# Retention layer with a routed MLP: another order of work on GpSimd, masks and one-hots on other engines, narrower state products

## The chip, the cores and the metric

The kernel runs on one core of a Trainium2 chip. The metric is device time in microseconds of one execution. The profile is a hardware trace of one execution; its span, from the first to the last instruction, is somewhat shorter than the device time. Five engines work from queues of their own, each in the order in which the program gives it the instructions: TensorE (PE; its weight loads are listed as PEld), VectorE (DVE), ScalarE (ACT), GpSimd (POOL) and SyncE (SP). DMA moves data between device memory and the on-chip buffer.

## What is computed

Four sequences (B = 4) of S = 768 positions with H = 8 heads of D = 64. Each head keeps a 64×64 state that decays by a constant of the head. The result, 512 wide, goes through a mixture-of-depths layer: of each sequence the 128 rows with the highest score pass an MLP (512 to 1024 to 512) and are added back, weighted by a sigmoid of the score; the others are left as they are.

```python
for t in range(S):
    state = gamma * state + k[t] (outer) v[t]          # per batch and head
    y[t] = scale * q[t] @ state
x = y as (B, S, H * D)
scores = x @ w_gate
for b in range(B):
    top = the 128 rows of x[b] with the highest score
    ye = relu(x[b, top] @ w1) @ w2
    out[b] = x[b];  out[b, top] += sigmoid(scores[b, top]) * ye
```

## The kernel before

The recurrence is done in chunks of 128 positions, two chunks to a block, 12 blocks, three to a sequence. Within a chunk the scores q·k are computed at once, masked to the causal half (`am`), and multiplied with v; what comes from earlier chunks is q times the state. The state is accumulated in a PSUM bank (`PS`) and copied to SBUF in bf16 (`St`) after each chunk.

All operations are entered into a plan: each has an engine, an estimated cost, what it reads and what it writes. A list scheduler in plain Python, which runs while the program is built, simulates the plan with these costs and so fixes the order on each engine. The order is static: on the chip nothing is rearranged.

```python
P.dma(0.87, ..., nc.gpsimd.dma_start(kt[:, m], ...))   # q, k, v: 36 loads by GpSimd, float32 to bf16
...
def prep(m):        # per block: kd = k * decay (DVE), transposes of kd and q (PE), their copies (ACT, DVE)
    ...
MASKED = {(m, 1, 1): ("tt" if m % 2 else "aff") for m in range(1, NBL)}   # NBL = 12
def block(m):       # four mask units a block: (half, s)
    f_qk: for hp, r, s, X:                              # 16 products a half, 64 rows x 64 columns each
        matmul(bank[A0 + s][X * 64:(X + 1) * 64, ...], kT[i][s * 64:.., ..64 columns], qT[i][s * 64:.., ..128])
    f_m:  am = bank * mask                              # DVE, all units that aren't in MASKED
    f_mc: am = copy of bank (ACT);  f_mp: am *= mask, or affine_select in two halves (POOL)
    f_kv: for hp, r:                                    # state, 8 products a chunk
        matmul(o[:, hp, :], kd[i][x, r, 2 * hp:2 * hp + 2, :], V[x, 2 * hp:2 * hp + 2, r, :])
    f_se: St = copy of bank[PS], two diagonal halves (ACT)
    f_qs: Y += qT @ St;  f_av: Y += am @ V              # PE
    f_xs: xs = scale * Y (ACT);  f_sc: score = sum(scale * Y * wg) (DVE)
```

In `f_kv` a product has the keys of two heads as its 128 columns and the values of the same two heads as its 128 moving columns, so it gives a 2×2 arrangement of 64×64 blocks of which the two diagonal ones are used.

The selection counts for each row how many rows of its sequence have a higher score (`L`, comparisons on DVE, counts on PE), builds one-hot matrices `OH` from the ranks, gathers the 128 rows with them on PE, and runs the MLP:

```python
def select(b, ...):
    cnt (PE) -> rk (DVE)
    def f_oh():
        e = nc.gpsimd if b < B - 1 else nc.vector
        for c in range(NC):                             # NC = 6
            e.tensor_scalar(OH[b % 2][:, c, :], slots, rk[..., c:c + 1], after[:, c:c + 1],
                            op0=OP.subtract, op1=OP.is_equal)
    ax (PE: row numbers and gates) ; xr (PE: rows) -> XR (ACT) -> transposes (PE) -> XG (ACT)
def mlp(b, ...):
    h (PE) -> hT = relu (ACT) -> ye (PE) -> ot = ye * gate + XR (DVE) -> scatter into out (POOL, indirect DMA)
...
AHEAD = 5           # loads of blocks 1 to 4 first, then one block ahead per block
if m == 0: ld_w("w1", ...); ld_w("w2", ...)             # weights: two loads of 1024 KB (bf16) each
```

Of the kernel before, what the change touches and what calls it, by code (L numbers as in the profile page):

```python
# [27 lines left out]
PE, DVE, ACT, POOL, SP, DMA = "PE", "DVE", "ACT", "POOL", "SP", "DMA"  # L28
LAT = {PE: 0.20, DVE: 0.16, ACT: 0.25, POOL: 0.2, SP: 0.1, DMA: 0.1}


class Op:
    __slots__ = ("i", "eng", "cost", "fn", "deps", "name", "succ", "due", "start", "end")


class Plan:


    def __init__(self):
        self.ops = []  # L40
        self.wr = {}
        self.rd = {}

    def add(self, eng, cost, fn, reads=(), writes=(), name="", due=None, after=()):
# [16 lines left out]
        o.succ = []  # L61
        self.ops.append(o)
# [4 lines left out]
    def dma(self, issue, nbytes, fn, reads=(), writes=(), name="", eng=POOL, rate=0.37, fixed=1.8, due=None):  # L67
        a = self.add(eng, issue, fn, reads=reads, writes=[("iss", name)] + list(writes), name=name, due=due)
        t = self.add(DMA, nbytes / rate / 1e6, None, reads=[("iss", name)], writes=[("fly", name)], name=name + ".x",
                     after=[])  # L70
        self.add("FLY", fixed, None, reads=[("fly", name)] + list(reads), writes=writes, name=name + ".f", after=[t])
        return a
# [6 lines left out]
    def forward(self, prio):  # L79
# [5 lines left out]
        free = {}  # L85
# [6 lines left out]
        while done < n:  # L92
            best = None
            for e, c in cand.items():
                if not c:
                    continue
                f = free.get(e, 0.0)
                if e == "FLY":
                    i = min(c, key=lambda i: ready[i])
                    t = ready[i]  # L100
                else:
                    t0 = max(f, min(ready[i] for i in c))
                    i = min((i for i in c if ready[i] <= t0 + 1e-9), key=lambda i: prio[i])
                    t = max(f, ready[i])
                if best is None or t < best[0]:
                    best = (t, e, i)
# [57 lines left out]
    def order(self, rounds=6, verbose=False):  # L164
        n = len(self.ops)
        tail = [0.0] * n
# [4 lines left out]
        for r in range(rounds):  # L171
            s, e = self.forward(prio)
            m = max(e)
            if verbose:
                print("forward", r, m)
            if best is None or m < best[0] - 1e-9:
                best = (m, s, e)
            prio = self.backward(e)
        m, s, e = best
        self.makespan, self.st, self.en = m, s, e  # L180
        return sorted(range(n), key=lambda i: (s[i], i))
# [3 lines left out]
def kernel(  # L185
# [13 lines left out]
    C = 128  # L199
# [80 lines left out]
    def load_k(m):  # L280
        P.dma(0.87, 2 * C * Dm * 4, lambda: nc.gpsimd.dma_start(kt[:, m], src_ap(k, m)), writes=[("k", m)],  # L281
              name=f"ldk{m}")

    def load_q(m):
        P.dma(0.87, 2 * C * Dm * 4, lambda: nc.gpsimd.dma_start(qt[:, m], src_ap(q, m)), writes=[("q", m)],  # L285
              name=f"ldq{m}")

    def load_v(m):
        P.dma(0.87, 2 * C * Dm * 4, lambda: nc.gpsimd.dma_start(vt[:, m], src_ap(v, m)), writes=[("v", m)],  # L289
              name=f"ldv{m}")  # L290
# [23 lines left out]
    for e, t in ((PE, 2.0), (DVE, .8), (ACT, 2.4), (POOL, 1.3), (SP, 1.0)):  # L314
        P.add(e, t, None, name="boot", due=-1.0)
    load_k(0)
    P.add(POOL, 0.2, c_tn, writes=["tn"], name="tn")
    P.add(POOL, 0.3, c_iota, writes=["jp"], name="jp")
    load_q(0)
    P.add(POOL, 0.94, c_tl, writes=["tl"], name="tl")  # L320
    load_v(0)
    P.add(POOL, 0.3, c_tk, writes=["tk"], name="tk")
# [21 lines left out]
    P.add(DVE, 0.6, c_mask, reads=["tl", "tn"], writes=["mask"], name="mask")  # L344
# [15 lines left out]
    for n in range(NB):  # L360
        P.add(ACT, 8 * .18, c_gk(n), reads=["tn"], writes=[("gk", n)], name=f"gk{n}")
        P.add(ACT, 4 * .37, c_gq(n), reads=["lg", "tl"], writes=[("gq", n)], name=f"gq{n}")
# [3 lines left out]
    for i in range(2):  # L366
        P.add(DVE, 0.4, c_S(i), writes=[("S", i, 0), ("S", i, 1)], name=f"S{i}z")
# [26 lines left out]
    P.add(DVE, 2.0, c_aux, reads=["tk"], writes=[("aux0", b) for b in range(B)], name="aux0")  # L394


    def prep(m):
# [28 lines left out]
        P.add(PE, .45, f_kt, reads=[("kd", i), "ident"], writes=[("b", TK)], name=f"KT{m}")  # L426
        P.add(ACT, .92, f_ke, reads=[("b", TK)], writes=[("kT", i)], name=f"ke{m}")
        P.add(PE, .48, f_qt, reads=[("q", m), "ident"], writes=[("b", TQ)], name=f"QT{m}")
        P.add(DVE, .6, f_qe, reads=[("b", TQ), ("gq", n)], writes=[("qT", i)], name=f"qe{m}")

    MASKED = {(m, 1, 1): ("tt" if m % 2 else "aff") for m in range(1, NBL)}

    def block(m):
# [4 lines left out]
        for half in range(2):  # L438
# [25 lines left out]
            def f_mp(s, ia=ia):  # L464
                def f():
                    if MASKED[m, half, s] == "tt":
                        nc.gpsimd.tensor_mul(am[ia][s].rearrange("p a r t -> p a (r t)"),  # L467
                                             am[ia][s].rearrange("p a r t -> p a (r t)"),
                                             mask.rearrange("p r t -> p (r t)")[:, None, :].to_broadcast([128, 2, 2 * C]))
                    else:  # L470
                        for X in range(2):
                            t = am[ia][s][X * 64:(X + 1) * 64].rearrange("p a r (u i) -> p a r u i", u=2)
                            nc.gpsimd.affine_select(t, t, pattern=[[0, 2], [-1, 2], [1, 2], [2, 64]], base=0,
                                                    channel_multiplier=-2, compare_op=OP.is_ge, fill=0.0)
                return f
            P.add(PE, 0.5, f_qk, reads=[("kT", i), ("qT", i)], writes=[("b", A0), ("b", A1)], name=f"qk{m}.{half}")
            for s in range(2):
                if (m, half, s) in MASKED:
                    P.add(ACT, 0.493, f_mc(s), reads=[("b", A0 + s)], writes=[("am", ia, s)], name=f"mc{m}.{half}{s}")
                    P.add(POOL, .95, f_mp(s), reads=[("am", ia, s), "mask"], writes=[("am", ia, s)],  # L480
# [5 lines left out]
        for X in range(2):  # L486
# [3 lines left out]
            def f_kv(X=X, c=c):  # L490
                o = bank[PS].rearrange("p (a x) -> p a x", a=HP)
                x = slice(X * P2, (X + 1) * P2)
                for hp in range(HP):
                    for r in range(2):
                        nc.tensor.matmul(o[:, hp, :], kd[i][x, r, 2 * hp:2 * hp + 2, :], V[x, 2 * hp:2 * hp + 2, r, :],  # L495
                                         start=(c == 0 and hp == 0 and r == 0), stop=False, skip_group_check=True)

            def f_se(s, c=c):
                def f():
                    nc.scalar.activation(  # L500
                        St[c % 2][s * 64:(s + 1) * 64, :, s, :],
                        bank[PS].rearrange("p (a s e) -> p a s e", a=HP, s=2)[s * 64:(s + 1) * 64, :, s], AF.Copy)
# [6 lines left out]
            if c:  # L509
                P.add(PE, .24, f_qs, reads=[("qT", i), ("S", (c - 1) % 2, 0), ("S", (c - 1) % 2, 1)],  # L510
                      writes=[("b", Y0 + X)], name=f"qs{j}")
            if c < NC - 1:
                P.add(PE, 0.46, f_kv, reads=[("kd", i), ("v", m)], writes=[("b", PS)], name=f"kv{j}")
                for s in range(2):
                    P.add(ACT, .28, f_se(s), reads=[("b", PS)], writes=[("S", c % 2, s)], name=f"se{j}.{s}")

        for half in range(2):
            for s in range(2):
# [13 lines left out]
                P.add(PE, 0.24, f_av, reads=[("am", ia, s), ("v", m)], writes=[("b", Y0), ("b", Y1)],  # L532
# [14 lines left out]
    def srow(js, bk):  # L547
# [6 lines left out]
        P.add(PE, n * .13, f, reads=[("sc", j) for j in js] + ["identf"], writes=[("b", bk)], name=f"sr{js[0]}")  # L554
# [6 lines left out]
        for a, j in enumerate(js):  # L561
# [6 lines left out]
            P.add(DVE, .08 + (c + 1) * .133, h, reads=[("SR", b % 2, cc) for cc in range(c + 1)] + [("sc", j), "tri"],  # L568
# [14 lines left out]
    def select(b, cnt, axb, xrb, xgb):  # L583
# [7 lines left out]
        P.add(PE, 21 * .05, f_cnt, reads=[("L", c) for c in range(NC)] + ["tri"], writes=[("b", cnt)], name=f"cnt{b}")  # L591
# [6 lines left out]
        def f_oh():  # L598
            e = nc.gpsimd if b < B - 1 else nc.vector
            for c in range(NC):  # L600
                e.tensor_scalar(OH[b % 2][:, c, :], slots, rk[b % 2][:, c:c + 1], after[:, c:c + 1],  # L601
                                        op0=OP.subtract, op1=OP.is_equal)
        P.add(POOL if b < B - 1 else DVE, 1.6 if b < B - 1 else .98, f_oh, reads=[("rk", b % 2), "slots", "after"], writes=[("OH", b % 2)], name=f"oh{b}")
# [5 lines left out]
        P.add(PE, .3, f_aux, reads=[("OH", b % 2), ("aux", b)], writes=[("b", axb)], name=f"ax{b}")  # L609
# [18 lines left out]
        P.add(PE, 1.35, f_xr, reads=[("OH", b % 2)] + [("xs", b * NC + c) for c in range(NC)], writes=[("b", xrb)],  # L628
# [15 lines left out]
    def mlp(b, hb, yb):  # L644
        for s in range(2):
# [6 lines left out]
            P.add(PE, .92, f_h, reads=[("XG", b % 2), "w1"], writes=[("b", hb[s])], name=f"h{b}.{s}")  # L652
# [5 lines left out]
        for s in range(2):  # L658
# [3 lines left out]
            P.add(PE, .88, f_y, reads=[("hT", b % 2, s), "w2"], writes=[("b", yb)], name=f"ye{b}.{s}")  # L662
# [3 lines left out]
        P.add(DVE, .62, f_o, reads=[("b", yb), ("g", b), ("XR", b)], writes=[("ot", b)], name=f"o{b}")  # L666
# [16 lines left out]
    def store(j0, n):  # L683
        b, c = divmod(j0, NC)

        def f():
            for r in range(2):
# [7 lines left out]
        P.dma(1.1, n * C * Dm * 4, f, reads=[("xs", j) for j in range(j0, j0 + n)], writes=[("out", b, c)],  # L695
              name=f"st{j0}")

    def ld_w(name, t, src, n, rows):
        P.dma(1.0, 128 * n * rows * 4, lambda: nc.gpsimd.dma_start(
            t, bass.AP(tensor=src.tensor, offset=src.offset, ap=[[rows, 128], [128 * rows, n], [1, rows]])),  # L700
            writes=[name], name="ld" + name)


    AHEAD = 5
    for m in range(1, AHEAD):
        load_block(m)
    prep(0)
    for m in range(NBL + 1):
# [3 lines left out]
        if m < NBL:  # L712
            block(m)
            if m + AHEAD < NBL:
                load_block(m + AHEAD)
            if m == 0:
# [59 lines left out]
```

## Time and profile before

| | |
|---|---|
| device time, median of 2 runs (lowest to highest) | 132.25 us (131.7 to 132.8) |
| span of the profiled execution | 129.8 us |
| DMA packets | 42753, 19.38 MB |
| loads of q, k and v | 36 issues of 256 KB (bf16), about 11 us each from issue to landing |
| loads of the weights | 2 issues of 1024 KB (bf16), 15.8 us |
| stores of the unchanged rows | 6 of 768 KB and 6 of 256 KB |
| mean granted TensorE clock | 0.828 |
| GpSimd: issues of the 36 loads | 32.9 us busy |
| GpSimd: one-hots, 18 of 24 | 14.3 us busy |
| GpSimd: masks, 6 multiplications and 10 half selections | 7.4 and 8.4 us busy |

How to read the profile: the page gives busy time and share of each engine, then the span in 40 equal slices with the busy share in tenths (9 is 90% or more), then the chain of work that ended last, followed back from the last instruction, then groups of instructions by source line. In a group's row, `out<-in` names the tiles, then come shapes, the count, busy time in us and the mean of one in ns, and behind the second bar the idle time of the engine just ahead of these instructions with what ended most of it. In a timeline's row the numbers ahead of the engine are start and duration in us; consecutive instructions of one kind are merged (x6). A busy PE isn't PE at its peak, as the ends of its pipelined matmuls are modelled.

### The profile page before, as it was taken

To read this page: it belongs to the slowest core of one execution; us is meant where nothing else is said; L and a number is where in the kernel's file an instruction comes from. 1 tells how busy PE (TensorE), PEld (TensorE's weight loads), DVE (VectorE), ACT (ScalarE), POOL (GpSimd) and SP (SyncE) were. 2 spreads that over 40 slices of the span, in tenths; PEclk is the share of its full clock that TensorE was granted. 3 is DMA by queue.
4 is the path that set the end of the run, shared out by engine and by line. 5 is a ranking of instruction groups with operands and counts; after the bars stand their busy time and mean duration, and the time that the engine had idled before them with its cause. 6 is when DMAs were issued, how large, how long until landed. Compare 5 with 4: busy or idle time off the path is not lost.

```text
span 129.8 us, 3889 instructions
## 1 busy us (share of the span) xinstructions
PE 92.4 (71%) x1621; PEld 67.4 (52%) x1628; DVE 82.0 (63%) x239; ACT 70.4 (54%) x156; POOL 78.3 (60%) x107
## 2 busy tenths in 40 slices
PE   0047997968773063998989866999999728799900
PEld 0045676757462042486758754388857514667500
DVE  2377746999993051856999993689995567601220
ACT  3879796697512070198576952549866521325300
POOL 6999656990565599999165598004579995000150
PEclk9999999999755555699999995589999755569995
DMA  0999999999999999999999940000888605000022
GB/s 1 140 165 175 181 222 181 190 216 189 182 181 186 205 194 181 181 182 182 181 222 405 405 110 0 3 5 0 248 251 248 218 18 158 8 0 0 0 81 81
DMA packets 42753, 19.38 MB, mean 149 GB/s; under 512 B 37744, under 2 KB 38768, under 8 KB 42736
## 3 DMA queue, kind: packets, MB, share of 16 engines
q0 software_dynamic: 42592, 18.88, 102.5%
q10 hardware_dynamic: 144, 0.26, 0.6%
q8 instruction: 12, 0.20, 0.6%
q14 instruction: 5, 0.04, 0.1%
HBM read 23.33 MB, written 7.34 MB: 236 GB/s over the span
## 4 chain that ended last, share of the span: by engine, by line
POOL 30%; PE 22%; DMA 18%; DVE 16%; issue 7%; ACT 3%; POOLq 1%; DVEq 0%
POOL OH L601 11%; DMA vt<-in_v_dram 10%; DMA qt<-in_q_dram 8%; PE bank L626 7%; DVE scr L541 4%; PE bank L649 4%; POOL qt L285 4%; DVE L L565 4%; DVE am L454 3%; POOL vt L289 3%; POOL kt L281 3%; POOL am L467 3%; DVE qT L424 3%; POOL out_dram L690 2%; ACT xs L538 2%
## 5 line engine op out<-in xcount | busy, mean ns | idle before, releaser
L454 DVE TENSOR_TENSOR am<-bank,mask 128x512 bf16<-128x512 f32 x37 | 24.2, 683 | 2.2 <-PE bank L447 2.0
L541 DVE SCALAR_TENSOR_TENSOR scr<-bank,wg 128x512 bf16<-128x512 f32 x24 | 16.5, 689 | 11.6 <-ACT xs L538 9.9
L538 ACT ACTIVATE xs<-bank 128x512 bf16<-128x512 f32 x24 | 13.5, 596 | 14.8 <-PE bank L527 11.9
L500 ACT ACTIVATE S<-bank 64x256 bf16<-64x256 f32 x40 | 15.1, 377 | 4.3 <-PE bank L495 3.5
L565 DVE SCALAR_TENSOR_TENSOR L<-SR,sc,tri 128x256 bf16<-128x256 f32 (+5 forms) x24 | 16.6, 706 | 0.3 <-ACT SR L557 0.2
L527 PE MATMUL bank<-vt,am 64*128 64x64 bf16 x384 | 11.9, 201 | 6.3 <-POOL am L467 5.6
L411 PE MATMUL bank<-ident,kd 128*128 128x128 bf16 x96 | 9.3, 254 | 8.9 <-DVE ident L332 8.3
L285 POOL DMA_DIRECT2D qt<-in_q_dram x12 | 10.9, 912 | 6.9 <-DMA w<-in_moe_w_dram 3.1
L601 POOL TENSOR_SCALAR OH<-slots,rk,after 128x128 bf16<-128x128 bf16 x18 | 14.3, 799 | 1.3 <-DVE rk L594 1.2
L421 ACT ACTIVATE kT<-bank 128x1024 bf16<-128x1024 bf16 x12 | 12.3, 1022 | 4.5 <-PE bank L411 4.4
L495 PE MATMUL bank<-vt,kd 64*128 64x128 bf16 x160 | 14.0, 235 | 0.4 <-ACT S L500 0.4
L447 PE MATMUL bank<-qT,kT 64*64 64x128 bf16 x384 | 12.6, 252 | 1.4 <-DVE qT L424 0.9
L670 POOL DMA_INDIRECT out_dram<-ot,idx x4 | 4.2, 1044 | 15.5 <-DVE ot L665 15.1
L467 POOL TENSOR_TENSOR am<-am,mask 128x512 bf16<-128x512 bf16 x6 | 7.4, 1230 | 9.7 <-ACT am L461 9.4
L527 PEld LDWEIGHTS <-am 64*128 64x128 bf16 x384 | 8.4, 100 | 9.0 <-POOL am L467 5.7
L281 POOL DMA_DIRECT2D kt<-in_k_dram x12 | 11.1, 921 | 2.8 <-DMA vt<-in_v_dram 1.4
L411 PEld LDWEIGHTS <-kd 128*128 128x128 bf16 x96 | 7.1, 115 | 10.2 <-DVE kd L402 9.5
L289 POOL DMA_DIRECT2D vt<-in_v_dram x12 | 10.9, 910 | 2.3 <-DMA qt<-in_q_dram 1.2
L424 DVE TENSOR_TENSOR qT<-bank,gq 128x1024 bf16<-128x1024 bf16 x12 | 8.2, 687 | 5.8 <-PE bank L418 4.5
L495 PEld LDWEIGHTS <-kd 64*128 64x128 bf16 x160 | 10.4, 103 | 2.5 <-issue 1.9
L690 POOL DMA_DIRECT2D out_dram<-xs x12 | 8.1, 674 | 5.9 <-ACT xs L538 5.8
L447 PEld LDWEIGHTS <-kT 64*64 64x64 bf16 x384 | 8.0, 122 | 5.2 <-issue 3.3
(63 smaller groups left out, 166.3 us busy)
## 6 DMA issues: line engine op xcount, KB each, us to landing
out_dram<-xs POOLq DMA_DIRECT2D x6, 768.0 KB, 10.1
kt<-in_k_dram POOLq DMA_DIRECT2D x12, 256.0 KB, 11.2
qt<-in_q_dram POOLq DMA_DIRECT2D x12, 256.0 KB, 11.1
vt<-in_v_dram POOLq DMA_DIRECT2D x12, 256.0 KB, 11.7
w<-in_moe_w_dram POOLq DMA_DIRECT2D x2, 1024.0 KB, 15.8
out_dram<-xs POOLq DMA_DIRECT2D x6, 256.0 KB, 3.4
wg<-in_moe_w_gate_dram ACTq DMA_DIRECT2D x1, 256.0 KB, 6.9
out_dram<-ot,idx POOLq DMA_INDIRECT x4, 3.0
```

The lines of the kernel that those rows point to most:

```text
L281: P.dma(0.87, 2 * C * Dm * 4, lambda: nc.gpsimd.dma_start(kt[:, m], src_ap(k, m)), writes=[("k", m)], name=f"ldk{m}")
L285: P.dma(0.87, 2 * C * Dm * 4, lambda: nc.gpsimd.dma_start(qt[:, m], src_ap(q, m)), writes=[("q", m)], name=f"ldq{m}")
L411: nc.tensor.transpose(tview(TK, hp)[:, :, r, :], kd[i][:, r, 2 * hp:2 * hp + 2, :], ident)
L447: nc.tensor.matmul(o[X * 64:(X + 1) * 64, hp, r, :], kT[i][s * 64:(s + 1) * 64, 2 * half + hp, X, r * 64:(r + 1) * 64], qT[i][s * 64:(s + ...
L454: nc.vector.tensor_mul(am[ia][s].rearrange("p a r t -> p a (r t)"), bank[A0 + s].rearrange("p (a x) -> p a x", a=2), mask.rearrange("p r t ...
L495: nc.tensor.matmul(o[:, hp, :], kd[i][x, r, 2 * hp:2 * hp + 2, :], V[x, 2 * hp:2 * hp + 2, r, :], start=(c == 0 and hp == 0 and r == 0), s ...
L500: nc.scalar.activation(St[c % 2][s * 64:(s + 1) * 64, :, s, :], bank[PS].rearrange("p (a s e) -> p a s e", a=HP, s=2)[s * 64:(s + 1) * 64, ...
L527: nc.tensor.matmul(bank[Y0 + X][:, h * 64:(h + 1) * 64], am[ia][s][x, hp, r, :], V[x, h, r, :], start=(n == 0 and X == 0 and half == 0 and ...
L538: nc.scalar.activation(xs[:, j, :], bank[Y0 + X], AF.Copy, scale=scale)
L541: nc.vector.scalar_tensor_tensor(scr, bank[Y0 + X], scale, wg, op0=OP.mult, op1=OP.mult, accum_out=sc[:, j:j + 1])
L565: nc.vector.scalar_tensor_tensor(L[c], SR[b % 2][:, 0:c + 1, :], sc[:, j:j + 1], tri[:, NC - 1 - c:, :], op0=OP.is_ge, op1=OP.mult, accum_ ...
L601: e.tensor_scalar(OH[b % 2][:, c, :], slots, rk[b % 2][:, c:c + 1], after[:, c:c + 1], op0=OP.subtract, op1=OP.is_equal)
```

## The change

It has six parts.

1. The planner learns that at most `RING = 6` loads or stores of GpSimd can be in flight, that loads are issued in a fixed order, and with costs nearer to those measured; so it can place an issue where it will not have to wait. All loads are entered ahead of the blocks. The search for an order runs 24 rounds with a fixed seed and some noise, and each candidate is replayed against four sets of jittered costs.
2. All one-hot matrices are built by VectorE.
3. 19 of the 48 mask units, not 11, go by ScalarE (copy) and GpSimd (multiplication); the half selections are gone.
4. The state products have 64 columns and 64 moving columns, one for each head: 16 a chunk. Only the diagonal blocks are computed.
5. The weights are loaded in eight parts, placed between the loads of blocks 2 to 6.
6. Products of zeros into an unused bank fill gaps that the plan shows on TensorE ahead of the first use of that bank.

What it is for: GpSimd's queue should not hold masks behind issues that can't proceed, and the three slow one-hot groups should leave GpSimd, which takes more masks instead; TensorE should have less to do for the state and keep its clock.

```diff
+RING = 6
+ROUNDS, SEED, NOISE = 24, 20, 0.3
+WARM = 0.6
...
+        if eng == POOL:
+            if len(self.ring) >= RING:
+                after.append(self.ring[-RING])
+            if fifo and self.last is not None:
+                after.append(self.last)
...
-    MASKED = {(m, 1, 1): ("tt" if m % 2 else "aff") for m in range(1, NBL)}
+    MASKED = {(m, 1, 1) for m in range(1, NBL - 1)} | {(m, 0, 1) for m in range(2, 11)}
...
-                    if MASKED[m, half, s] == "tt":
-                        nc.gpsimd.tensor_mul(am, am, mask)
-                    else:
-                        for X in range(2):
-                            nc.gpsimd.affine_select(t, t, ...)
+                    nc.gpsimd.tensor_mul(am, am, mask)
...
-                o = bank[PS].rearrange("p (a x) -> p a x", a=HP)
+                o = bank[PS].rearrange("p (a e) -> p a e", e=D)
                 for hp in range(HP):
                     for r in range(2):
-                        nc.tensor.matmul(o[:, hp, :], kd[i][x, r, 2 * hp:2 * hp + 2, :], V[x, 2 * hp:2 * hp + 2, r, :], ...)
+                        for s in range(2):
+                            nc.tensor.matmul(o[s * 64:(s + 1) * 64, hp, :], kd[i][x, r, 2 * hp + s, :],
+                                             V[x, 2 * hp + s, r, :], ...)
...
-            e = nc.gpsimd if b < B - 1 else nc.vector
             for c in range(NC):
-                e.tensor_scalar(OH[b % 2][:, c, :], ...)
+                nc.vector.tensor_scalar(OH[b % 2][:, c, :], ...)
...
-    AHEAD = 5
-    for m in range(1, AHEAD):
+    WAT = [2, 3, 3, 4, 4, 5, 5, 6]
+    for m in range(1, NBL):
         load_block(m)
+        for i in range(8):
+            if WAT[i] == m:
+                ld_w(i)
...
+    zero = St[1].rearrange("p a s d -> p (a s d)")
+    def warm(n):
+        for _ in range(n):
+            nc.tensor.matmul(bank[M], zero[:, 0:128], zero, start=True, stop=True)
...
+        if o.eng == PE and o.fn is not None:
+            gap = P.st[i] - pe_end
+            if gap > 0.4 and P.st[i] < first_m:
+                warm(int(WARM * gap / 0.22))
```

## The prediction

> **What bounds the kernel now.** I read the page from the top: the shares, the 40 slices, the chain that ended last, the groups; then the waits, then the timelines of GpSimd, TensorE and VectorE, then busy time by stretches.
>
> ```profile
> span 129.8 us, 3889 instructions
> PE 92.4 (71%) x1621; PEld 67.4 (52%) x1628; DVE 82.0 (63%) x239; ACT 70.4 (54%) x156; POOL 78.3 (60%) x107
> ...
> PE   0047997968773063998989866999999728799900
> PEld 0045676757462042486758754388857514667500
> DVE  2377746999993051856999993689995567601220
> ACT  3879796697512070198576952549866521325300
> POOL 6999656990565599999165598004579995000150
> PEclk9999999999755555699999995589999755569995
> DMA  0999999999999999999999940000888605000022
> ```
>
> No engine is over 71% busy, so no engine alone is the bound. The DMA engines are full until about 72 us and then nearly idle, and the chain's 18% of DMA lies there; but 55 us of computing follow. PE falls to 0 in the 14th slice, to 3 in the 16th and to 2 in the 33rd; DVE dips beside it, while POOL shows 9 in the 16th and the 33rd, and 5 in the 14th. The clock row falls to 5 three times, about these holes and a smaller one in the 25th slice (the first time a few us ahead of the hole, where PE already had short gaps). So the suspicion is GpSimd. The chain agrees:
>
> ```profile
> POOL 30%; PE 22%; DMA 18%; DVE 16%; issue 7%; ACT 3%; POOLq 1%; DVEq 0%
> ```
>
> The GpSimd timeline around the first hole shows in what order that queue worked:
>
> ```profile
> 40.79 0.87 POOL L289 DMA_DIRECT2D vt<-in_v_dram  x1 [0.55 <-DMA vt<-in_v_dram]
> 43.57 0.87 POOL L285 DMA_DIRECT2D qt<-in_q_dram  x1 [1.91 <-DMA kt<-in_k_dram]
> 44.51 1.15 POOL L467 TENSOR_TENSOR am<-am,mask 128x512 bf16<-128x512 bf16 x1
> 45.60 0.94 POOL L289 DMA_DIRECT2D vt<-in_v_dram  x1
> 46.59 4.68 POOL L601 TENSOR_SCALAR OH<-slots,rk,after 128x128 bf16<-128x128 bf16 x6
> ```
>
> The bracket is what ended the idle time ahead of a row: load issues waited for an older load to land. The 14th bulk load (14.80 us) is the first that waited; by then about 8 could have landed at the 1.41 us a load takes (0.262 MB written at some 186 GB/s), so about six are in flight at once. The mask multiply L467 had its input from ScalarE at 36.0 us and stood behind five such issues until 44.51. TensorE, which needs that mask, has nothing from 40.1 to 45.71. Then the one-hot matrices: 4.68 us on GpSimd, six TensorE steps waiting for one each.
>
> ```profile
> 39.90:45.70 5.80, 0.24 (x8) 0.08 (x4) 0.65 (x1) 0.00 (x0) 3.28 (x5) 0.50 1.48 198
> 45.70:51.30 5.60, 2.67 (x37) 1.90 (x37) 2.00 (x5) 2.32 (x5) 5.55 (x8) 0.50 1.65 187
> 51.30:74.70 23.40, 21.72 (x437) 16.28 (x440) 19.69 (x48) 15.77 (x31) 15.40 (x17) 0.93 1.72 250
> 102.60:107.40 4.80, 1.88 (x27) 1.16 (x21) 2.07 (x6) 1.58 (x3) 4.80 (x7) 0.50 0.36 102
> ```
>
> (Stretch and length, then busy us of PE, PEld, DVE, ACT, POOL, the clock, DMA, GB/s.) In the third stretch, which has no such hole, DVE is 84% busy. That is the kernel when nothing blocks it.
>
> **What the Trainium skill says.** "TensorE: Matmul & The Clock Gate", section "What's actually happening": the array runs at half rate until it has been busy for about 3.4 us, and falls back after an idle window. The trace agrees in direction: eight transposes take 1.01 us at 8.28 and 0.62 us at 26.40, and 0.50 stands in the clock column in and after the holes (in the first 20 us that column says 1.00 though the matmuls are slow, so there the durations decide). "TensorEngine Tiling (Array Packing)", section "Key Properties": tiles of the array run in parallel. The trace agrees: 16 score products of 64 rows and 64 columns take 0.42 us, with 128 moving columns each, while 8 state products of 64 rows and all 128 columns take 0.62. "SBUF — State Buffer", section "SBUF: two separate sides": VectorE operations with two SBUF inputs and GpSimd operations block each other. The trace agrees: the largest comparison on DVE takes 1.01 us mostly and 1.43 at 67.86, where a pair of GpSimd selections takes 2.35 us instead of 1.45.
>
> **The change part by part.**
>
> ```profile
> L454 DVE TENSOR_TENSOR am<-bank,mask 128x512 bf16<-128x512 f32 x37 | 24.2, 683 | 2.2 <-PE bank L447 2.0
> ...
> L601 POOL TENSOR_SCALAR OH<-slots,rk,after 128x128 bf16<-128x128 bf16 x18 | 14.3, 799 | 1.3 <-DVE rk L594 1.2
> L495 PE MATMUL bank<-vt,kd 64*128 64x128 bf16 x160 | 14.0, 235 | 0.4 <-ACT S L500 0.4
> ...
> L467 POOL TENSOR_TENSOR am<-am,mask 128x512 bf16<-128x512 bf16 x6 | 7.4, 1230 | 9.7 <-ACT am L461 9.4
> ```
>
> 1. Load pacing. The planner gets the limit of six in flight, so a mask is put ahead of an issue that would block. Removes the hole of 45.71 − 40.1 = **5.6 us**, all on the path. The loads themselves are bytes and remain: 9.4 MB of q, k, v and 2.1 MB of weights as bf16, 11.5 MB at 186 GB/s = 62 us, ending near 66 us in both. The weights only change their place: 8 issues of about 0.8 us for 2, +5 us of GpSimd that lie beside other work.
>
> 2. One-hots on VectorE. Six there already took 1.43 us for the last batch (111.60), against 4.7. Three batches save 3.3 us each on the way rank, one-hot, gather: about **10 us** of path if the queue behind stood still, as it did twice fully (45.7 and 102.6) and once in part (74.7, where 2.5 us of matmul ran beside it). I count 8. DVE pays 3 × 1.43 = +4.3 us.
>
> 3. Masks. 19 units by ScalarE and GpSimd instead of 11: DVE −8 × 0.65 = −5.2, ACT +8 × 0.6 = +4.8 (0.5 at their start distance), GpSimd 19 × 1.2 = 23 for 7.4 + 8.4 = 15.8, +7. With part 2 DVE stays at 82; GpSimd goes 78 − 14 + 7 + 5 = 76; ACT 75. So this buys room for part 2 and little by itself; it lengthens the way from score to masked score from 0.6 to 1.9 us, which other blocks' work should hide.
>
> 4. State products. 16 of 64 columns, in pairs on two column halves, for 8 of 128. By the pattern above (64×64 tiles) a group should take about 0.2 + 16 × 0.0135 = 0.41 for 0.62; −0.2 × 20 = −4 us of PE, of which I put **1 to 2** on the path.
>
> 5. Zero matmuls. From 8 to 20 us the matmuls are at half speed: some 10 us of PE busy that would be 5 to 6. But loads, exponentials on ACT and masks on DVE pace this start, so I count **1**.
>
> 6. The clock after the holes. The holes go, and with them the half rate behind them: 45.9 to 55.3, 80 to 85.4 and 103 to 116 hold about 5, 5 and 10 us of matmul at half rate, half of which is loss, so 10 us of PE; I put **5** on the path.
>
> Sum: 5.6 + 8 + 1.5 + 1 + 5 = 21; 129.8 − 21 = **109** us of span.
>
> **The check from below.** VectorE's 82 us need not shrink. About 2.5 of it come before the first load lands at 7.4 us, about 5 belong to the last batch's selection; 74.5 remain. At the 84% to 90% that the unblocked stretch shows the last score falls at 7.4 + 74.5 / 0.87 = 93 (at 100%: 82). The tail behind it, at full clock and alone, from the rows of the last batch: transposed scores 0.4, their copy 0.4, last two comparisons 1.75, counts 0.75, rank 0.2, one-hots 1.45, gather of 6 about 1.7, copy 0.6, transposes 0.4, copy 0.6, first layer 1.1 + 1.0, copy 0.6, second layer 1.0, with handovers 0.7: 12.7; from the start of ot to the end the trace has 129.8 − 123.6 = 6.2. Together 19, against 24.5 now. 93 + 19 = 112. Two ways give 109 and 112; PE, at about 4.1 us a block and 6 a batch, asks for nearly as much as DVE, so bubbles between the two are to be expected. I take 109 for the span's lower reading and 112 for the upper, 110.5 between them; a timed run is 2.4 us above the span (132.25 against 129.8), hence near 113, from which I take two for the new order's search, which also tries its orders against jittered costs: **111 us**.
>
> **Rivals.** (a) VectorE becomes the bound and GpSimd's larger share blocks it through the shared port. For it: 82 us unchanged, and 1.43 against 1.01. Against: only some DVE forms have two SBUF inputs. It would end at 116 to 119. (b) The load stream remains the bound. For it: DMA is full to 66 us. Against: block 11's first operation starts at 83.0, long after its data; and the tail holds no load. If all computing kept up, the end would be 66 + 8 + 19 + 2.4 = 95, which is thus the floor and out of reach. (c) The issues still block GpSimd, because landing times differ from the planned 1.48 us; masks, now 19, stand behind them. For it: 11.2 us median from issue to landing, the plan is static. It would give back up to the 5.6 us and put the time at 116. (d) The zero matmuls stand in the way of real ones: 0.43 us each when cold. They come only where the plan has a gap; worst case 2 us.
>
> **Range and chances.** Rivals (a), (c) and (d) give the upper side, an order with fewer bubbles (DVE at 95%: 7.4 + 78 + 19 + 2.4 = 107) the lower; below 105 DVE would have to run without any gap. Range 105 to 118. For no gain at all, 21 us of visible holes and half clock would have to come back elsewhere: 2% for within 2%, 1% for slower.
>
> **What would show it.** No PE slice at 0 before the last two; the clock column at 0.50 not before the tail; no L601 row on POOL and 24 on DVE at some 0.24 us apart; L467 x19 with mean 1.2 to 1.4; a state group (16 products) near 0.42 us; the last load landed by 68; DVE at 72% or more of a span of 108 to 109; transposes of block 0 at 0.6 us. The prediction is wrong if GpSimd issues still wait for DMA with a mask behind them, if L454 or L565 rows lengthen by over 10%, or if the stretch after the last load is as sparse as now.

## The result, and the profile after

The changed kernel takes 123.04 us (123.02 to 123.07, 2 runs) against 132.25 (131.7 to 132.8): 0.930 of before, interval 0.914 to 0.947. It is faster, but 12 us above the predicted 111 and outside the range of 105 to 118. Ranges and ratios below are, unless said otherwise, of the executions within 1.5% of the fastest of their kernel in the same set, since the slower ones mostly had a lower granted TensorE clock; the profile of before, with its 0.828, was of the slower kind, and within that limit before took 128 to 131 us. Beside before once more (run 15 below) the changed kernel took 122.7 to 124.0 us against 129.9 to 131.1, 0.945 (0.933 to 0.956); so the gain is nearer to 7 us than to 9.

The page of the changed kernel, its shares and slices:

```profile
span 121.2 us, 4278 instructions
PE 93.2 (77%) x1821; PEld 63.5 (52%) x1821; DVE 91.0 (75%) x249; ACT 73.8 (61%) x164; POOL 75.6 (62%) x98
...
PE   3948559757967939999939849999799569699910
...
DVE  3936779796996799552999999979979996971220
...
PEclk9999999997699995589999995589999955899999
DMA  0999999999999999999999929999949980600112
```

The zero of the 14th slice is gone. But DVE, predicted to stay at 82 us, is 91 us busy, in a shorter span. The chain of waits names it too: POOL had 30% of it and has 4%, DVE had 16% and now has 33%.

```profile
DVE 33%; PE 31%; ACT 11%; issue 10%; DMA 6%; POOL 4%; POOLq 1%; DVEq 0%; ACTq 0%
DVE L L598 12%; DVE scr L574 8%; PE bank L658 7%; DMA kt<-in_k_dram 6%; DVE kd L439 5%; DVE am L491 4%; PE bank L448 4%; PE bank L681 3%; ACT S L533 3%; PE bank L484 3%; PE bank L455 3%; PE bank L560 3%; ACT xs L571 2%; ACT am L498 2%; PE bank L527 2%
```

Which of DVE's operations grew is in its groups by shape (count, then busy us and mean ns of one), first two of before, then those of the changed kernel:

```profile
L402 DVE TENSOR_TENSOR kd<-kt,gk 128x1024 bf16<-128x1024 bf16 x12 | 8.3, 688 | 0.9 <-PE bank L495 0.9
...
L565 DVE SCALAR_TENSOR_TENSOR L<-SR,sc,tri 128x768 bf16<-128x768 f32 x4 | 4.5, 1120 | 0.1
```

```profile
L491 DVE TENSOR_TENSOR am<-bank,mask 128x512 bf16<-128x512 f32 x29 | 19.4, 683 | 2.2 <-PE bank L484 2.1
L574 DVE SCALAR_TENSOR_TENSOR scr<-bank,wg 128x512 bf16<-128x512 f32 x24 | 16.5, 686 | 4.0 <-ACT xs L571 2.3 <-PE bank L560 0.9
L439 DVE TENSOR_TENSOR kd<-kt,gk 128x1024 bf16<-128x1024 bf16 x12 | 10.4, 866 | 1.1 <-DMA kt<-in_k_dram 1.1
...
L598 DVE SCALAR_TENSOR_TENSOR L<-SR,sc,tri 128x768 bf16<-128x768 f32 x4 | 6.4, 1600 | 0.7 <-ACT SR L590 0.6
...
L598 DVE SCALAR_TENSOR_TENSOR L<-SR,sc,tri 128x640 bf16<-128x640 f32 x4 | 5.5, 1384 | 0.0
```

The masks and scores, whose first input is a PSUM bank, take what they took before (masks 683 ns in both, scores 686 after 689). `kd` and the comparisons, which read two tensors in SBUF, have gone from 688 to 866 and, for 128x768, from 1120 to 1600. The timelines of the two engines show what stood beside the longest ones. First VectorE, then GpSimd, start and duration in us:

```profile
25.91 1.94 DVE L439 TENSOR_TENSOR kd<-kt,gk 128x1024 bf16<-128x1024 bf16 x1
...
42.41 2.02 DVE L598 SCALAR_TENSOR_TENSOR L<-SR,sc,tri 128x640 bf16<-128x640 f32 x1
```

```profile
26.13 1.16 POOL L503 TENSOR_TENSOR am<-am,mask 128x512 bf16<-128x512 bf16 x1
...
42.57 1.17 POOL L503 TENSOR_TENSOR am<-am,mask 128x512 bf16<-128x512 bf16 x1
```

The mask multiplication ends at 27.29, and `kd` ends 0.56 us later; the comparison ends 0.69 us after the multiplication that ends at 43.74. Alone they take 0.68 and 0.88. So most of such an operation's own time lies behind the end of the multiplication: by these times the two don't share, one waits. Eleven of the 19 multiplications held up a `kd` or a comparison in this way. It goes both ways: six multiplications took 1.23 to 1.65 us instead of 1.15, and each ended 1.01 or 1.02 us after the `kd` or comparison that was under way when it began. This is rival (a) of the prediction, larger than it was put there. One of the signs that the prediction had named for being wrong is there: the row of all comparisons (L565 before, L598 now) rose from a mean of 706 to 960 ns, by 36%, where 10% was the limit.

### The profile page after: what moved, and what is told of

It is laid out like the page before. It is cut to its first block, busy times and chain, and to the rows that moved or that the text cites. A ratio compares the mean times of both kernels' runs of the same rounds, so it can differ in the third digit from the quotient of the medians.

```text
span 121.2 us, 4278 instructions
## 1 busy us (share of the span) xinstructions
PE 93.2 (77%) x1821; PEld 63.5 (52%) x1821; DVE 91.0 (75%) x249; ACT 73.8 (61%) x164; POOL 75.6 (62%) x98
## 4 chain that ended last, share of the span: by engine, by line
DVE 33%; PE 31%; ACT 11%; issue 10%; DMA 6%; POOL 4%; POOLq 1%; DVEq 0%; ACTq 0%
DVE L L598 12%; DVE scr L574 8%; PE bank L658 7%; DMA kt<-in_k_dram 6%; DVE kd L439 5%; DVE am L491 4%; PE bank L448 4%; PE bank L681 3%; ACT S L533 3%; PE bank L484 3%; PE bank L455 3%; PE bank L560 3%; ACT xs L571 2%; ACT am L498 2%; PE bank L527 2%
## 5 line engine op out<-in xcount | busy, mean ns | idle before, releaser
L503 POOL TENSOR_TENSOR am<-am,mask 128x512 bf16<-128x512 bf16 x19 | 23.6, 1244 | 22.3 <-ACT am L498 19.8
L598 DVE SCALAR_TENSOR_TENSOR L<-SR,sc,tri 128x128 bf16<-128x128 f32 (+5 forms) x24 | 22.5, 960 | 3.4 <-ACT SR L590 3.4
L491 DVE TENSOR_TENSOR am<-bank,mask 128x512 bf16<-128x512 f32 x29 | 19.4, 683 | 2.2 <-PE bank L484 2.1
L777 PE MATMUL bank<-S 128*128 128x512 bf16 x33 | 10.8, 450 | 3.9 <-ACT S L533 2.0
L448 PE MATMUL bank<-ident,kd 128*128 128x128 bf16 x96 | 8.2, 234 | 6.4 <-DVE kd L439 6.4
L498 ACT ACTIVATE am<-bank 128x512 bf16<-128x512 f32 x19 | 11.4, 598 | 2.0 <-PE bank L484 1.7
L560 PE MATMUL bank<-vt,am 64*128 64x64 bf16 x384 | 10.9, 199 | 1.0 <-DVE am L491 1.0
L324 POOL DMA_DIRECT2D qt<-in_q_dram x12 | 10.9, 912 | 0.7 <-DMA kt<-in_k_dram 0.7
L439 DVE TENSOR_TENSOR kd<-kt,gk 128x1024 bf16<-128x1024 bf16 x12 | 10.4, 866 | 1.1 <-DMA kt<-in_k_dram 1.1
L448 PEld LDWEIGHTS <-kd 128*128 128x128 bf16 x96 | 6.1, 104 | 8.5 <-DVE kd L439 7.9
L540 PE MATMUL bank<-S,qT 128*128 128x128 bf16 x80 | 8.0, 227 | 2.5 <-ACT xs L571 1.3
```

Of the source, the lines that this page charges most:

```text
L439: nc.vector.tensor_mul(kd[i], kt[:, m].rearrange("p h (r d) -> p r h d", r=2), gk[:, n])
L448: nc.tensor.transpose(tview(TK, hp)[:, :, r, :], kd[i][:, r, 2 * hp:2 * hp + 2, :], ident)
L491: nc.vector.tensor_mul(am[ia][s].rearrange("p a r t -> p a (r t)"), bank[A0 + s].rearrange("p (a x) -> p a x", a=2), mask.rearrange("p r t ...
L498: nc.scalar.activation(am[ia][s].rearrange("p a r t -> p (a r t)"), bank[A0 + s], AF.Copy)
L560: nc.tensor.matmul(bank[Y0 + X][:, h * 64:(h + 1) * 64], am[ia][s][x, hp, r, :], V[x, h, r, :], start=(n == 0 and X == 0 and half == 0 and ...
L598: nc.vector.scalar_tensor_tensor(L[c], SR[b % 2][:, 0:c + 1, :], sc[:, j:j + 1], tri[:, NC - 1 - c:, :], op0=OP.is_ge, op1=OP.mult, accum_ ...
```

## Experiments

**1. GpSimd writes, but doesn't read.** Theory P: the multiplications on GpSimd hold VectorE's operations with two SBUF inputs, and that is the lost time. Rivals: the static order, or the longer way of those masks. The order is kept; only what GpSimd does to the tile changes, so 19 units go unmasked. (Shortened; the original line has reshaped views of the two tiles.)

```diff
-  nc.gpsimd.tensor_mul(am, am, mask)
+  nc.gpsimd.memset(am, 0.01)
+  nc.gpsimd.memset(am, 0.01)
```

> The changed kernel in the same order, but each of the 19 GpSimd mask multiplications is replaced by two fills of the same tile with a constant: GpSimd writes the tile and reads none, so the masks are left out of those units and the values are not the reference's. The chain ScalarE copy, GpSimd, TensorE stays. Theory P (VectorE operations that read two SBUF tensors are held up while a GpSimd multiplication reads SBUF; this cost the 9 us by which VectorE's busy time exceeds the predicted 82): the kd row falls from a mean of 866 ns to about 690, the comparison row from 960 to about 710, VectorE busy from 91 to 82 or 83 us, and the time from 123.0 to 112 to 115 us. Rival O (the static order and the wait for ScalarE's copies pace the kernel, VectorE's longer operations fill what would be idle anyway): busy time falls but the time stays within 121 to 123 us. Rival W (any GpSimd access to SBUF, writes too, holds VectorE): rows and time stay as in the changed kernel, if the fills last as long as the multiplications.

112.4 us, 0.867 of before (0.861 to 0.872). Its DVE groups and page:

```profile
L597 DVE SCALAR_TENSOR_TENSOR L<-SR,sc,tri 128x128 bf16<-128x128 f32 (+5 forms) x24 | 15.7, 679 | 3.5 <-ACT SR L589 3.4
...
L439 DVE TENSOR_TENSOR kd<-kt,gk 128x1024 bf16<-128x1024 bf16 x12 | 8.2, 684 | 1.1 <-DMA kt<-in_k_dram 1.1
```

```profile
PE 90.6 (82%) x1821; PEld 61.4 (56%) x1821; DVE 80.4 (73%) x249; ACT 73.6 (67%) x164; POOL 71.3 (65%) x117
```

And GpSimd's timeline where the multiplication of 26.13 was:

```profile
26.31 0.55 POOL L503 MEMSET am<- 128x512 bf16 x1
26.92 0.53 POOL L504 MEMSET am<- 128x512 bf16 x1
```

The two fills last 1.14 us together, as long as an unhindered multiplication (1.15), and stand in the same chain, so GpSimd's time and the latency of a mask have hardly changed. VectorE is back at 80.4 us and the kernel 10.7 us faster. Theory P holds; the rival that any GpSimd access holds VectorE falls for operations with two SBUF inputs (a small `aux` operation with one did take 0.40 us for 0.17 beside a fill). The mean granted clock rose as well, from 0.900 to 0.937; that this alone brought the time is unlikely, since the third run, at 0.817, takes no longer than the changed kernel's later executions. How much of the gain comes by way of the clock isn't separated. "SBUF — State Buffer", section "SBUF: two separate sides", in the Trainium skill says this: the port pair is locked for a whole instruction, and a VectorE operation with two SBUF inputs contends only with a GpSimd operation that reads SBUF. The measurement agrees, with 1.94 us for 0.68 at the worst.

**2. The multiplications left out**, so that ScalarE's copy goes straight to TensorE.

> The changed kernel in the same order without the 19 GpSimd mask multiplications: those units go unmasked from ScalarE's copy to TensorE, so the values are not the reference's. This takes away the port conflict and also 23.6 us of GpSimd work and 1.2 us of latency in each of 19 chains, and the load issues behind the masks come earlier. Theory P: no more than 2 us faster than the run in which GpSimd only writes, so 111 to 114 us. Rival L (the longer way from score to masked score, or the load issues that stand behind masks, is what costs): clearly faster than the write-only run, by 4 us or more. Rival O: 120 us or more in both.

VectorE is 80.2 us busy, as in the first run. One execution took 112.6 us and three others 116.0 to 116.7. It is not faster than the write-only kernel, so the longer way of a mask costs nothing that shows.

**3. No zero matmuls** (`WARM = 0.0`).

> The changed kernel in the same order without the zero matmuls (33 of them, 10.8 us of TensorE busy in the profile). If they do what the prediction put on them, the first 10 to 15 us run at half speed and the time rises by 1 us to about 124. If they do nothing for the time it stays at 123.0 plus or minus 0.3. If they stand in the way of real matmuls (the profile has single ones that waited for ScalarE's state copy) it falls by 1 to 2 us.

123.2 and 123.7 us: 0.2 to 0.7 more than the 123.0 of the changed kernel, and within the 122.7 to 124.0 of its later executions, so no gain from the zeros is shown. The first eight transposes take 1.03 us instead of 0.62: the zeros do speed up these matmuls, as predicted, but that this start paces the kernel doesn't show. Its TensorE timeline:

```profile
7.19 1.03 PE L448 MATMUL bank<-ident,kd 128*128 128x128 bf16 x8 [7.19 <-DVE kd L439]
```

**4. State products of 128 columns again.**

```diff
-  for s in range(2): matmul(o[s * 64:(s + 1) * 64, hp, :], kd[i][x, r, 2 * hp + s, :], V[x, 2 * hp + s, r, :])
+  matmul(o[:, hp, :], kd[i][x, r, 2 * hp:2 * hp + 2, :], V[x, 2 * hp:2 * hp + 2, r, :])
```

> The changed kernel in the same order with the state products as before: 8 of 128 columns and 128 moving columns a chunk instead of 16 of 64. A group should take 0.62 us instead of 0.44 at full clock. Prediction's step 4 (1 to 2 us on the path): 124 to 125 us. If VectorE and not TensorE paces the blocks: 123.0 to 123.5 us.

124.4 to 125.8 us, about 2 more than the changed kernel. There a group of 16 narrow products took 0.44 us where the matmuls are fast (0.41 predicted), against 0.62 for the 8 wide ones of before. Step 4 of the prediction holds at its upper end.

**5 and 6. No mask unit, or 11, on GpSimd** (`MASKED = set()`; `MASKED = {(m, 1, 1) for m in range(1, NBL)}`), planned anew.

> The changed kernel with no mask unit on ScalarE and GpSimd: all 48 on VectorE, the order planned anew. The output is the reference's. VectorE gets 19 x 0.65 = 12 us more of masks and, by theory P, loses the 9 us for which GpSimd's multiplications held it: busy 94 us for 91, comparison row back at a mean near 710 ns, kd near 690, and a time of 123 to 127 us, so that moving the masks away from VectorE was worth almost nothing. Rival (the holding costs little, the masks moved do help): 130 us or more.

> The changed kernel with 11 mask units on ScalarE and GpSimd for 19 (one a block, as before), the order planned anew. Output as the reference's. VectorE +8 x 0.65 = +5 us of masks, and by theory P about 8/19 of the 9 us of holding away, -4: 122 to 125 us. If the holding grows faster than the number of masks, 118 to 121.

With none: 123.4 to 125.2 us; with 11: 120.7 at best, 122.5 to 124.3 otherwise. With none VectorE is 91.9 us busy, and its comparison and `kd` rows are back at 679 and 686 ns. So 12 us of masks taken from VectorE bought about 1 us, no more than another order of the same kernel brings (runs 12 to 15): what VectorE no longer computes it waits for. With 11, VectorE is 89.6 us busy and the comparison row at 769 ns; that 19 masks are better than 11 isn't shown.

**7. A planner that knows of the conflict.** One more resource, `PORT`, in the list scheduler and the replay, which a GpSimd mask and VectorE's `kd`, comparisons and `aux` can't hold at once.

```diff
+  if self.ops[i].port:
+      t = max(t, free.get("PORT", 0.0))
```

> The changed kernel with the planner told that a GpSimd mask multiplication and VectorE's kd, comparison and aux operations exclude each other in time (one more resource in the list scheduler and the replay); everything else equal, 24 rounds, same seed. Output as the reference's. Theory P, and the static order holds on the chip: comparison and kd rows come down most of the way, VectorE busy 84 to 86, 115 to 119 us. If jitter brings the two together again: busy near 90 and 121 to 124 us.

120.9 and 122.0 us, and VectorE 90.1 us busy: the conflict is hardly less (comparison row 986 ns, `kd` 805). The order that avoids it in the plan doesn't avoid it on the chip. A reason is at hand, not shown: the order fixes sequence, not time.

**8. Pacing undone** (`RING = 99`).

> The changed kernel with the planner's limit of loads in flight set to 99, so that it places issues as if none ever waited; the rest equal, order planned anew. Prediction's step 1 (pacing is worth 5.6 us): GpSimd waits at load issues with masks behind them, 126 to 130 us. If the pacing does nothing, because VectorE paces the kernel: 122 to 124.5 us.

127.8 to 129.5 us, 5 more than the changed kernel. That is the size of step 1 (5.6), though not one hole: GpSimd waits at single load issues, 1.8 us at most, and the order is another one, so not all of the 5 us need be pacing.

**9 and 10. One-hots.** Back on GpSimd in the changed kernel's order; and, in the kernel before, on VectorE as the only change.

```diff
 # 9, in the changed kernel
-  nc.vector.tensor_scalar(OH, ...)
+  (nc.gpsimd if b < B - 1 else nc.vector).tensor_scalar(OH, ...)
 # 10, in the kernel before
-  e = nc.gpsimd if b < B - 1 else nc.vector
+  e = nc.vector
```

> The changed kernel in the same order with the one-hots of the first three batches back on GpSimd (18 operations of about 0.8 us). VectorE loses 4.3 us, GpSimd gains 14. Prediction's step 2 (about 8 us of path): 129 to 132 us. If VectorE is the only thing that counts: 119 to 123 us, as its busy time falls.

> The kernel before with one part alone: all one-hots on VectorE, the order planned anew by its own planner. Few masks run on GpSimd there, so little is held. Prediction's step 2: 8 us less than before on the same chip, so about 122 to 124 us. If the holes merely move (a load issue blocks GpSimd elsewhere): 127 us or more.

The ninth: 129.3 to 131.2 us, 1.000 of before (0.995 to 1.005). In this order, which was not planned for one-hots on GpSimd, the change gains nothing without this one part; it is worth some 7 us there, near the 8 of step 2. The tenth: 126.2 to 128.1, 0.986 (0.980 to 0.991), only 2 us. Alone, and planned anew, the part brings little: TensorE now waits some 8 us, in seven pieces, for masks of GpSimd, which still stops at load issues, once for 4.1 us. The gain of a part depends on what else has been removed, and on the order.

**11 and 14. A version without the conflict.** All masks on VectorE; comparisons between different chunks as signs of differences, with their sum, on ScalarE; VectorE keeps the diagonal ones. Counts and ranks are doubled (sign is ±1), so `slots` counts in steps of 2.

```diff
...
-  nc.vector.scalar_tensor_tensor(L[c], SR[:, 0:c + 1, :], sc_j, tri[:, NC - 1 - c:, :], is_ge, mult, accum_out=R1)
+  nc.vector.scalar_tensor_tensor(L[c][:, c, :], SR[:, c, :], sc_j, tri[:, NC - 1, :], is_ge, mult, accum_out=R1)
+  nc.scalar.activation(L[c][:, 0:c, :], SR[:, 0:c, :], AF.Sign, bias=sc_j, scale=-1.0, accum_out=R1a)
...
```

> A version meant to keep the gain without the conflict: no mask on GpSimd (all 48 on VectorE), and the comparisons of different chunks go to ScalarE as the sign of a difference with its sum, so VectorE compares only the diagonal 128x128 part; ranks are counted doubled, the output is the reference's. By theory P VectorE has 92 us (all masks on it) less some 9 for the comparisons, 83, held by nothing; ScalarE 64 + 12 = 76 us: 112 to 117 us. If VectorE's load is not what sets the pace: 120 us or more, near the version with all masks on VectorE.

> The version with comparisons by sign on ScalarE and no mask on GpSimd, with 240 search rounds for 24 and the sign operations' cost raised to what was measured (0.38 + 0.107 a chunk). Output as the reference's. If its order was at fault: 113 to 118 us. If ScalarE, which now does the comparisons between the scores and the ranks, paces it: 120 to 123 us as before.

121.0 to 122.5 us, and with 240 search rounds 120.6 to 121.1, 0.925 of before (0.917 to 0.932). It beats both kernels, by 2 to 3 us against the changed one, but falls short of 113 to 118. The page of the latter:

```profile
PE 96.8 (81%) x1819; PEld 64.6 (54%) x1819; DVE 84.2 (71%) x273; ACT 77.2 (65%) x185; POOL 51.4 (43%) x79
```

VectorE has 84 us as planned, 7 less than in the changed kernel, and the time falls by only 2 to 3. VectorE has 4 us more than in the write-only kernel, ScalarE 4 us more as well. So VectorE's busy time alone doesn't set the time of every version.

**12, 13 and 15. Is it the order?** Another seed (`SEED = 21`) for the changed kernel and for the write-only one, and the changed kernel again beside them.

> The changed kernel with seed 21 for 20 in the search for an order, nothing else. If the order found is of little weight: 122 to 124.5 us. If seed 20 was a lucky one: 126 us or more.

> The write-only kernel (GpSimd fills instead of multiplying, masks of those units left out) with seed 21. If the conflict is the cause of the 11 us, and not a match of one order with it, this is 9 to 12 us faster than the changed kernel with seed 21 and has VectorE busy 80 to 82 us. If it is a matter of order: within 4 us of it.

> The changed kernel once more, on the chip of these runs: 122.5 to 124 us, VectorE busy 91 us.

Changed kernel: 122.7 to 124.0 us; with seed 21: 121.4 to 123.0, VectorE 91.3 us busy; write-only with seed 21: 112.0 and 113.0, VectorE 80.7. The two orders differ by 1 to 2 us; the conflict is worth 9 to 11 in both.

**16. Signs, and 11 masks on GpSimd.**

> The sign version with 11 mask units back on ScalarE and GpSimd, 240 search rounds. Output as the reference's. VectorE 84 - 7 + 2 = 79 us (what GpSimd can hold is now kd and the short diagonal comparisons), ScalarE 77 + 6 = 83 us. If VectorE paces the sign version: 115 to 118 us. If ScalarE does: 121 to 125 us.

122.8 and 123.2 us, 0.942 of before (0.930 to 0.953), some 2 us slower than without these masks. ScalarE rose from 77.2 to 83.1 us, but VectorE fell only from 84.2 to 82.8, not to 79: its short comparisons rose from 346 to 483 ns. So the conflict came back, and the run doesn't tell whether ScalarE holds the sign version; no run has taken work from ScalarE alone, and it remains open.

## Why the prediction was wrong

The step that failed is step 3, with its sentence "With part 2 DVE stays at 82". The list of operations was right: unheld, VectorE is 80.4 us busy in the first experiment. But 19 multiplications on GpSimd lengthen what VectorE has left by 91.0 − 80.4 = 10.6 us, or 0.56 us for each. The page of before had shown it, 1.43 us for 1.01 beside a GpSimd operation, and the prediction quoted it; it then named the blocking as a rival of 5 to 8 us and entered zero in the sum. A rough estimate could have been made from numbers of before: 19 multiplications of 1.2 us, and operations with two SBUF inputs (`kd` 8.3, comparisons 16.6 us) for 30% of VectorE's busy time, so 19 × 1.2 × 0.30 = 7 us. These two kinds lost 9.0 us; the rest of the 10.6 are mostly single small operations.

The check from below failed by the same term. Busy time between the first load and the last score (PE, PEld, DVE, ACT, POOL), first in the changed kernel, then in the write-only one:

```profile
6.40:104.10 97.70, 78.66 (x1686) 55.04 (x1686) 80.68 (x211) 63.53 (x136) 67.96 (x81) 0.88 1.32 184
```

```profile
6.40:93.16 86.76, 75.61 (x1688) 52.83 (x1686) 70.05 (x210) 63.38 (x136) 63.68 (x100) 0.94 1.48 207
```

The prediction had put 74.5 us of VectorE at 87% and the last score at 93. It was 80.7 us at 83%, and 104.1; without the conflict 70.1 at 81%, and 93.2. The two stretches differ by 10.9 us and VectorE's busy time in them by 10.6: the stretch grew by about as much as VectorE lost. That the write-only kernel meets the predicted 93 is in part luck: 74.5 was too high (in the profile of before, too, only 72.1 us lie between these two points) and 87% too dense, and the two errors cancel. The tail behind the last score, put at 19, took 17.1.

The other steps, by the runs: pacing 5.6, measured 5; one-hots 8, measured 7 in the changed kernel and 2 alone; state products 1 to 2, measured 2; zero matmuls 1, measured 0.2 to 0.7, which is within the scatter. The last load was not issued until 73.4 us instead of 58.5, as masks now stand between load issues, and ahead of masks GpSimd waited 19.8 us in all for ScalarE's copies; so "ending near 66 us in both" was wrong too. Only one `kd` waited for its load, 1.1 us early on, so this cost little. For step 6 no run stands alone: the clock column at 0.50 was predicted not before the tail, and it shows 5 in three stretches still. The write-only kernel's 112.4 us are near the predicted 111, so for a kernel without the conflict the sum was not far off; but beside before in the same set (129.7) that is a gain of 17 us and not 21, and part of the nearness comes from the high 132.25 at which the sum began.

## What to carry to other kernels

When work moves from one engine to another to relieve the first, ask what the two share besides data: here each multiplication given to GpSimd cost VectorE 0.56 us of the 0.65 it saved. Look for operations of one shape whose durations differ in the trace and set the other engine's timeline beside the long ones; then estimate how many such meetings there will be after the change. A fill in place of a multiplication, in the same order, tells such a conflict from latency and order in one run.

## What was not expected of the hardware

Waiting, not sharing, and in both directions: a `kd` of 0.68 us took 1.94 beside a GpSimd multiplication, and a multiplication of 1.15 us took up to 1.65 beside VectorE's operations. Which of the two waits doesn't follow from the recorded starts: one `kd` began 0.22 us ahead of a multiplication (26.13) and was held, another began 0.20 us ahead of one (54.51) and wasn't; there the multiplication took 1.49. A small `aux` operation of 6 columns, some 0.17 us, took 1.06 beside a multiplication, though it has one SBUF tensor as input; why isn't shown. Operations with a PSUM input were not lengthened (masks 683 to 685 ns in all kernels). Filling 128x512 in bf16 on GpSimd takes 0.53 us and held no `kd` or comparison. A planner told of the conflict did not avoid it, with 90.1 us busy for 91.0.
